# Top-32 attention with a SwiGLU block: ScalarE's part of the next two weight pieces put in front of exp

## The chip, the core and the metric

The kernel runs on one core of a Trainium2 chip. The core's engines run side by side, each through its own list of instructions in a fixed order, and wait for each other by semaphores: TensorE (PE in the profile; its weight loads are PEld), VectorE (DVE), ScalarE (ACT), GpSimd (POOL), and SyncE (SP), which here issues the transfers. The metric is the device time of one execution in microseconds, as the median over several executions. The time before is 1890.77 us (three executions, 1890.12 to 1893.95). The profile is of one further execution, whose span is 1892.5 us.

## The reference

Eight batches of eight heads, 576 positions, head size 64. Each row of scores keeps its 32 largest; the result, with the heads side by side, is the input of a feed-forward block of width 512 and inner width 1536.

```python
scores = scale * np.matmul(q, k.transpose(0, 1, 3, 2))
kth = np.partition(scores, -top_k, axis=-1)[..., -top_k:-top_k + 1]
scores = np.where(scores >= kth, scores, -1000000000.0)
attn = np.exp(scores - np.max(scores, axis=-1, keepdims=True))
attn = attn / (np.sum(attn, axis=-1, keepdims=True) + 1e-09)
x = np.matmul(attn, v)            # then (B,H,S,D) -> (B*S, H*D)
g = x @ w_gate
out = (g * (1.0 / (1.0 + np.exp(-g))) * (x @ w_val)) @ w_out
```

Here `top_k` is 32. The three weights come as 64-bit floats, each a low and a high 32-bit word, and everything is computed in 32-bit floats.

## The kernel before

**Units.** The attention is cut into 160 units `(b, qt, hp)`: a batch, a tile of 128 queries (or the last 64, a unit with half the work), and a pair of heads. The main loop is a software pipeline over units, and the program order of every engine is the order in which this loop writes its instructions down (a last pass ties each engine to it). In turn `n` of the loop:

- `penalize(n-1)` on GpSimd: a bias (L338) and the sum of scores and penalty (L340, 128x1152, the longest of GpSimd);
- `turn(n-3)`: transposes of the weights of attention on TensorE (L376) and their copies on ScalarE (L377); `finish_unit(n-4)`: the product with v (L396, L405) and the copy to `xT` (L420);
- the first step of `scores(n+1)`: matmuls (L297);
- `weigh(n-1)` on ScalarE: two exps with their row sums (L349) and a small addition (L354). It waits for L340;
- the rest of `scores(n+1)`: four copies of scores from PSUM on ScalarE (L302);
- `select(n)` on VectorE, step by step through `dve`: four rounds of MAX8 (L318) with three of MATCH_REPLACE8 (L322) for two heads, and at the end the penalties (L328). Between the steps stand pieces of the feed-forward block (`pieces`), the reciprocal and the scaling of unit `n-2` (`normalize`, L361 and L364), and steps of the weight pieces.

**Weight pieces.** Because the weights are 64-bit floats, the kernel itself turns them into 32-bit floats while the first units run. There are 72 pieces of 128x256; the generator `weights()` advances several of them by one step each in every one of its turns. `rounding(k)` runs k turns of it. `dve` calls `rounding(1)` in 5 of 11 of its counted steps, which is 4.5 pieces for a full unit. A piece goes through `rounded`:

1. SyncE loads it into `w`, a low and a high word for each element (L109);
2. ScalarE takes the absolute value of the high word (L114, into `size`); GpSimd clamps it (L116); ScalarE scales the low word by 2^-29 into a whole number (L119, into `ulps`);
3. VectorE shifts and masks `size` (L123); GpSimd adds `ulps` to it as whole numbers (L126);
4. VectorE puts the sign and top bit of the high word to it (L129). That is the finished weight, in `wg`, `wv` or `wo`.

The list `lags = (5, 3, 2, 0)` says how far apart these steps are: turn `n` finishes piece `n-5`, does step 3 of piece `n-3`, step 2 of piece `n-2`, and starts the transfer of piece `n`. So in every turn GpSimd has the addition L126 of piece `n-3` ahead of the clamp L116 of piece `n-2`, and VectorE has L129 ahead of L123. `size` has 4 buffers, `ulps` 2, `w` 6. Once all pieces are done, the same buffers hold differences of `wo` that the later blocks use (`t3`, `t2`, `t4`).

**Feed-forward blocks.** 18 blocks of 256 rows (`feed`), each a generator of small pieces of TensorE's work; `credit` sets how many of them a unit gets. A product's PSUM tile is emptied by ScalarE: for the gate a tanh, a halving and an addition (L484 to L486), for the value a copy (L491). The products with the gate and with the value are on GpSimd (L487, L492). Both kinds of work are put into the lists `on_act` and `on_pool`, and are written down when `flush` is called. The first block multiplies plainly by `w_out` (L505); the others use seven smaller products. `need` runs further turns of `weights()` if a block asks for a weight that isn't ready.

Before the loop:

```python
load(0)
rounding(4)
load(1)
run(fetch(0))
run(scores(0))
run(fetch(1))
```

Of the kernel before, what the change touches and what calls it, by code (L numbers as in the profile page):

```python
# [9 lines left out]
ALU = mybir.AluOpType  # L10
FP32 = mybir.dt.float32
I32 = mybir.dt.int32
U32 = mybir.dt.uint32
PSUM = bass.MemoryType.PSUM

P = 128
# [4 lines left out]
BLK = 256  # L21
# [6 lines left out]
def kernel(  # L28
# [37 lines left out]
    nc = tc.nc  # L66
    B, H, S, D = q.shape
    DM, DFF = w_gate.shape
# [6 lines left out]
    MS = MC // 2  # L75
# [10 lines left out]
    conv = ctx.enter_context(tc.tile_pool(name="conv", bufs=2))  # L86
# [18 lines left out]
    def rounded(src, dst):  # L105

        n = dst.shape[1]
        w = ffn.tile([P, n, 2], I32, tag="w", name="w", bufs=6)
        nc.sync.dma_start(w[:], src.bitcast(I32).rearrange("p (f t) -> p f t", t=2))  # L109
        yield  # L110
        low, high = w[:, :, 0], w[:, :, 1]

        size = conv.tile([P, n], FP32, tag="size", name="size", bufs=4)
        nc.scalar.activation(size[:], high.bitcast(FP32), AF.Abs)  # L114

        nc.gpsimd.tensor_scalar(size[:], size[:], HUGE, LEAST, ALU.min, ALU.max)  # L116

        ulps = conv.tile([P, n], I32, tag="ulps", name="ulps")
        nc.scalar.mul(ulps[:], low.bitcast(U32), 2.0**-29)  # L119
        yield  # L120

        bits = size[:].bitcast(I32)
        nc.vector.tensor_scalar(  # L123
            bits, bits, 3, 0x3FFFFFFF, ALU.logical_shift_left, ALU.bitwise_and
        )
        nc.gpsimd.tensor_tensor(bits, bits, ulps[:], ALU.add)  # L126
        yield

        nc.vector.scalar_tensor_tensor(  # L129
            out=dst.bitcast(I32), in0=high, scalar=-0x40000000, in1=bits,  # L130
            op0=ALU.bitwise_and, op1=ALU.bitwise_or,
        )

    def weights():

        pieces = []
        for f in range(0, DFF, WP):
            for src, dst in ((w_gate, wg), (w_val, wv)):
                for c in range(KC):
                    pieces.append((src[c * P : (c + 1) * P, f : f + WP], dst[:, c, f : f + WP]))  # L140
        for c in range(MC):
            for f in range(0, DM, WP):
                pieces.append((w_out[c * P : (c + 1) * P, f : f + WP], wo[:, c, f : f + WP]))
        pieces = [rounded(*p) for p in pieces]
        lags = (5, 3, 2, 0)
        for n in range(len(pieces) + lags[0]):
            for lag in lags:
                if 0 <= n - lag < len(pieces):
                    next(pieces[n - lag], None)
            ready[0] = max(n - lags[0] + 1, 0)  # L150
            yield


        add, sub = ALU.add, ALU.subtract
        lo, hi = slice(0, DM // 2), slice(DM // 2, DM)
        for m in range(0, MQ, 2):
            mm, nn = slice(m, m + 2), slice(MQ + m, MQ + m + 2)
            t3 = ffn.tile([P, 2, DM // 2], FP32, tag="w", name="t3", bufs=6)
            nc.gpsimd.tensor_tensor(t3[:], wo[:, nn, hi], wo[:, mm, hi], sub)
            T[7] += [t3[:, i, :] for i in range(2)]  # L160
            yield
        while not plain_done:
            yield
        for m in range(0, MQ, 2):
            mm, nn = slice(m, m + 2), slice(MQ + m, MQ + m + 2)
            t1 = wo[:, mm, hi]
            nc.gpsimd.tensor_tensor(t1, t1, wo[:, mm, lo], sub)
            T[5] += [wo[:, m + i, hi] for i in range(2)]
            yield
            t2 = ffn.tile([P, 2, DM // 2], FP32, tag="w", name="t2", bufs=6)  # L170
            nc.gpsimd.tensor_tensor(t2[:], wo[:, nn, hi], t1, sub)
            T[6] += [t2[:, i, :] for i in range(2)]
            yield
            for i in range(2):
                tag, bufs = ("size", 4) if m + i < 4 else ("ulps", 2)
                t4 = conv.tile([P, DM // 2], FP32, tag=tag, name="t4", bufs=bufs)
                nc.gpsimd.tensor_tensor(t4[:], wo[:, MQ + m + i, lo], t2[:, i, :], sub)
                T[4].append(t4[:])
            yield
        T[1] += [wo[:, m, lo] for m in range(MQ)]  # L180
        T[2] += [wo[:, MQ + m, lo] for m in range(MQ)]
        T[3] += [wo[:, MQ + m, hi] for m in range(MQ)]
        yield

    ready = [0]
    plain_done = []
    T = {i: [] for i in range(1, 8)}
    weight = weights()

    def rounding(n):  # L190
        for _ in range(n):
            next(weight, None)
# [70 lines left out]
    def n_heads(qt):  # L263

        return 1 if qt == J else 2
# [179 lines left out]
    def feed(kb):  # L445
# [5 lines left out]
        hs = []  # L451

        def product(w, s, then):
# [14 lines left out]
                yield 1  # L468

        plain = kb == 0  # L470
        early, late = slice(0, P), slice(P, BLK)

        s32 = x[:].rearrange("p a b -> p (a b)")[:, 0 : MQ * P].rearrange(
            "p (m t) -> p m t", t=P
        )
# [57 lines left out]
        def quarter(i, ps):  # L533
            for m in range(MQ):
                s, r = m // 2, m % 2
                lhsT = {
                    1: lambda: hs[s][:, r, early],
                    2: lambda: hs[s + MS // 2][:, r, early],
                    3: lambda: hs[s][:, r, late],
                    4: lambda: hs[s + MS // 2][:, r, late],  # L540
                    5: lambda: hs[s][:, r, late],
                    6: lambda: s32[:, m],
                    7: lambda: s32[:, m],
                }[i]()
                nc.tensor.matmul(  # L545
                    ps, lhsT, T[i][m], start=m == 0, stop=m == MQ - 1
                )
                if m % 3 == 2:
                    yield 0.75

        for s in range(MS // 2):
            nc.gpsimd.tensor_tensor(
                s32[:, 2 * s : 2 * s + 2], hs[s][:, :, early], hs[s][:, :, late], ALU.subtract
            )
        yield from quarter(1, y_ps[:, 0])
        flush(on_act)
# [6 lines left out]
        yield from quarter(7, x_ps[:, 1])  # L563
        for s in range(MS // 2):
            nc.gpsimd.tensor_tensor(
                s32[:, 2 * s : 2 * s + 2], hs[s][:, :, late], hs[s][:, :, early], ALU.subtract
            )
        yield from quarter(5, x_ps[:, 0])
        a = ffn.tile([P, 2, DH], FP32, tag="gv", name="p57", bufs=3)
# [22 lines left out]
        for s in range(MS // 2):  # L592
            nc.gpsimd.tensor_tensor(
                hs[s][:, :, late],
                hs[s + MS // 2][:, :, early],
                s32[:, 2 * s : 2 * s + 2],
                ALU.subtract,
            )
# [50 lines left out]
    def fetch(n):  # L649

        b, qt, hp = units[n]
        i = b * NHP + hp
        if qt == 0:
            yield from prep(i)
        if qt == J and i + NHP < len(pairs):
            load(i + NHP)
# [6 lines left out]
    def run(steps):  # L663
        for _ in steps:
            pass
# [5 lines left out]
            load_v((b + 1) * NHP + hp)  # L671

    load(0)
    rounding(4)
    load(1)
    run(fetch(0))
    run(scores(0))
    run(fetch(1))
    credit = [0.0]
    no = iter(())  # L680
# [3 lines left out]
    for n in range(NU + VALUES):  # L684
        nh = n_heads(units[n][1]) if n < NU else 1
        topk = select(n) if n < NU else no
        over[n - 1] = normalize(n - 1) if 0 <= n - 1 < NU else no
        nxt = scores(n + 1) if n + 1 < NU else no
        ahead = fetch(n + 2) if n + 2 < NU else no
        norm = over.pop(n - 2, no)  # L690

        def dve(k, beside=True):

            for _ in range(k * nh):
                next(topk, None)
                due[0] += 5 / 11 if beside else 0
                if due[0] >= 1:
                    due[0] -= 1
                    rounding(1)

        if n >= NU - NHP:
            credit[0] = 8.0
        else:
            credit[0] = min(credit[0] + (4.45 if nh == 2 else 2.25), 8.0)
        flush(on_act)
        if 0 <= n - 1 < NU:
            penalize(n - 1)
        flush(on_pool)
        if 0 <= n - TURN < NU:
            run(turn(n - TURN))  # L710
        if n >= VALUES:
            finish_unit(n - VALUES)
        next(nxt, None)
        if 0 <= n - 1 < NU:
            weigh(n - 1)
        run(nxt)

        dve(2, beside=False)
        if 2 <= n + 2 < NHP:
            load(n + 2)  # L720
        if n < NHP:
            load_v(n)
        pieces(2)
        flush(on_act)
        flush(on_pool)
        dve(1)
        dve(1)
        next(norm, None)
        run(norm)
        next(ahead, None)  # L730
        pieces(1)
        next(ahead, None)
        dve(1)
        pieces(1)
        dve(2)
        run(topk)
        pieces(6)
# [50 lines left out]
```

## Time and profile before

| | |
|---|---|
| time, median of 3 | 1890.77 us |
| span of the profiled execution | 1892.5 us |
| TensorE busy | 1723.2 us, 91% |
| VectorE busy | 1632.0 us, 86% |
| ScalarE busy | 1212.3 us, 64% |
| GpSimd busy | 1023.2 us, 54% |
| first and last Abs of a weight piece (L114) | 7.3 and 246.8 us |
| medians of L114, L116, L119, L123, L126, L129, us | 0.446, 0.400, 0.442, 0.288, 0.726, 0.41 |
| time that ScalarE waited before exp for L340 | 114.6 us in 49 waits, 66.2 of them before 480 us |

The profile's groups and waits are per engine: a busy time is a sum of the durations of instructions, and an idle time stands with the instruction that ended it and, behind an arrow, the one that released it. The timeline has a line for each instruction or run of like instructions: start, duration, engine, source line, operation, output and inputs, and in brackets the idle time before. Durations of neighbours on one engine overlap a little, so that the distance from start to start is shorter than the duration: two MAX8 of 0.75 us each together take 1.41.

### The profile page before, as it was taken

The numbers are of one execution on the slowest core, as the hardware profiler recorded it, in microseconds if no ns is written. First come the engines' busy times: TensorE is split into PE (matmuls) and PEld (weight loads), VectorE is DVE, ScalarE is ACT, GpSimd is POOL, SyncE is SP. The second block draws the span as 40 slices with busy tenths as digits, with TensorE's granted clock in tenths as the row PEclk, the third lists the DMA queues.
The fourth block names the chain that finished last, engine by engine and source line by source line (L and its number), as shares of the span: only waits on it lengthen the run. The fifth ranks groups of instructions, "written<-read, shape, count | busy, mean of one in ns | idle before, by whom it ended". The sixth has DMA issues, their size and how long they took to land.

```text
span 1892.5 us, 30875 instructions
## 1 busy us (share of the span) xinstructions
PE 1723.2 (91%) x10756; PEld 1419.1 (75%) x10756; DVE 1632.0 (86%) x3477; ACT 1212.3 (64%) x3015; POOL 1023.2 (54%) x1007
## 2 busy tenths in 40 slices
PE   3446789989999999899899999999999999899998
PEld 2335658868888878787788888878888878787877
DVE  7998789999999989997899989999899989999300
ACT  5656666667666666675667666766676767666531
POOL 4555656636455546555364655554646554546534
PEclk7668899989999999899999999999999999999989
DMA  7222212000300012000210003000210001000000
GB/s 186 84 84 78 67 27 69 1 12 2 78 12 12 1 28 64 12 1 13 52 38 1 12 3 82 7 12 1 53 38 12 1 14 46 18 1 12 1 12 12
DMA packets 111260, 59.67 MB, mean 32 GB/s; under 512 B 89088, under 2 KB 97280, under 8 KB 111104
## 3 DMA queue, kind: packets, MB, share of 16 engines
q1 hardware_dynamic: 109904, 57.41, 11.6%
q8 instruction: 85, 1.39, 0.3%
q14 instruction: 71, 0.58, 0.1%
q10 hardware_dynamic: 1200, 0.30, 0.1%
HBM read 48.23 MB, written 9.44 MB: 30 GB/s over the span
## 4 chain that ended last, share of the span: by engine, by line
PE 79%; ACT 7%; POOL 7%; DVE 4%; issue 2%; DMA 0%; SPq 0%; POOLq 0%; ACTq 0%
PE f L459 38%; PE av L405 8%; PE x_ps L545 8%; PE etps L376 8%; PE s L297 6%; PE y_ps L545 5%; POOL e L340 3%; ACT e L349 2%; PE s L283 2%; ACT sc L302 2%; PE av L396 1%; DVE m L318 1%; DVE rest L322 1%; PE kqps L252 1%; PE o_ps L505 1%
## 5 line engine op out<-in xcount | busy, mean ns | idle before, releaser
L318 DVE MAX8 m<-rest 128x8 f32<-128x576 f32 x864 | 615.2, 747 | 2.2
L322 DVE MATCH_REPLACE8 rest<-m,rest 128x576 f32<-128x576 f32 x576 | 423.9, 742 | 0.0
L340 POOL TENSOR_TENSOR e<-e,sc 128x1152 f32<-128x1152 f32 (+1 forms) x160 | 382.7, 2392 | 59.4 <-DVE e L328 59.0
L459 PE MATMUL f<-xT,wg 128*128 128x256 f32 x1728 | 404.8, 385 | 0.0
L459 PE MATMUL f<-xT,wv 128*128 128x256 f32 x1728 | 397.9, 381 | 0.0
L459 PEld LDWEIGHTS f<-xT,wg 128*128 128x128 f32 x1728 | 324.4, 191 | 66.7 <-issue 23.7
L459 PEld LDWEIGHTS f<-xT,wv 128*128 128x128 f32 x1728 | 324.3, 190 | 55.6 <-issue 13.5
L487 POOL TENSOR_TENSOR h<-h,half_g 128x512 f32<-128x512 f32 x108 | 138.0, 1278 | 385.9 <-ACT h L486 377.4
L318 DVE MAX8 m<-sc 128x8 f32<-128x576 f32 x288 | 205.4, 749 | 127.1 <-ACT sc L288 70.9
L376 PE MATMUL etps<-ident,e 128*128 128x128 f32 (+1 forms) x1312 | 191.0, 291 | 132.2 <-POOL size L116 48.1
L349 ACT ACTIVATE e<-e,bias 128x576 f32<-128x576 f32 x288 | 222.0, 776 | 114.6 <-POOL e L340 114.6
L376 PEld LDWEIGHTS etps<-ident,e 128*128 128x128 f32 (+1 forms) x1312 | 161.9, 150 | 163.9 <-POOL size L116 51.3
L377 ACT COPY et<-etps 128x512 f32<-128x512 f32 (+1 forms) x448 | 185.0, 483 | 126.5 <-PE etps L376 124.9
L492 POOL TENSOR_TENSOR h<-h,val 128x512 f32<-128x512 f32 x108 | 140.0, 1296 | 160.8 <-ACT val L491 160.8
L364 ACT ACTIVATE e<-e,tot 128x576 f32<-128x576 f32 x288 | 211.5, 787 | 5.3 <-DVE tot L361 5.1
L322 DVE MATCH_REPLACE8 rest<-m,sc 128x576 f32<-128x576 f32 x288 | 211.8, 741 | 0.0
L297 PE MATMUL s<-kqT 64*128 64x288 f32 x1024 | 175.5, 451 | 9.1 <-ACT kqT L257 5.8
L328 DVE TENSOR_SCALAR e<-sc,m 128x576 f32<-128x576 f32 x288 | 173.4, 639 | 3.4
L405 PE MATMUL av<-et,v 128*64 128x128 f32 (+1 forms) x2560 | 176.3, 284 | 0.0
L302 ACT COPY sc<-s 128x288 f32<-128x288 f32 x512 | 163.9, 402 | 3.3 <-PE s L297 3.3
L484 ACT ACTIVATE h<-f 128x512 f32<-128x512 f32 x108 | 65.2, 603 | 149.8 <-PE f L459 149.8
L405 PEld LDWEIGHTS av<-et,v 128*64 128x64 f32 x2560 | 139.2, 147 | 23.4 <-issue 7.9
(71 smaller groups left out, 2042.6 us busy)
## 6 DMA issues: line engine op xcount, KB each, us to landing
kq_in<-in_k_dram SPq DMA_DIRECT2D x64, 128.0 KB, 2.8
v<-in_v_dram SPq DMA_DIRECT2D x32, 256.0 KB, 3.0
kq_in<-in_q_dram SPq DMA_DIRECT2D x62, 128.0 KB, 2.9
w<-in_moe_w_gate_dram SPq DMA_DIRECT2D x24, 256.0 KB, 2.7
w<-in_moe_w_val_dram SPq DMA_DIRECT2D x24, 256.0 KB, 2.7
w<-in_moe_w_out_dram SPq DMA_DIRECT2D x24, 256.0 KB, 2.6
out_dram<-o SPq DMA_DIRECT2D x40, 128.0 KB, 2.4
out_dram<-o SPq DMA_DIRECT2D x16, 256.0 KB, 2.4
```

What stands on the lines that cost most here:

```text
L297: nc.tensor.matmul(ps[:, 0:half], slab[d, q0 : q0 + P], slab[d, k0 : k0 + half])
L302: nc.scalar.copy(sc[:, i * half : (i + 1) * half], ps[:, 0:half])
L318: nc.vector.max(m[:, t, 8 * r : 8 * r + 8], cur[:, hs])
L322: nc.vector.match_replace(rest[:, hs], m[:, t, 8 * r : 8 * r + 8], cur[:, hs], LOWEST)
L340: nc.gpsimd.tensor_tensor(e[:, every], e[:, every], sc[:, every], ALU.add)
L349: nc.scalar.activation(e[:, hs], e[:, hs], AF.Exp, bias=bias[:, t : t + 1], scale=scale, accum_out=tot[:, t : t + 1],)
L364: nc.scalar.mul(e[:, hs], e[:, hs], tot[:, t : t + 1])
L376: nc.tensor.transpose(ps[0:kl, c * P : (c + 1) * P], e[:, k0 : k0 + kl], ident[:])
L377: nc.scalar.copy(et[0:kl, c0 : c0 + cn, :], ps[0:kl, 0 : cn * P].rearrange("p (c j) -> p c j", c=cn),)
L405: nc.tensor.matmul(av[hh * R : (hh + 1) * R, 0:ql], v_last[:, hh, :] if c == J else vt[:, hh, c, :], moving, start=last and c == 0, stop=c ...
L459: nc.tensor.matmul(ps[:, i, :], w[:, kc, m * P : (m + 1) * P], x[:, kc, :], start=(kc == 0), stop=(kc == KC - 1),)
L545: nc.tensor.matmul(ps, lhsT, T[i][m], start=m == 0, stop=m == MQ - 1)
```

## The change

ScalarE's two instructions of a piece (L114 and L119) become a step of their own, ahead of the clamp. At the head of each unit, just before `weigh` writes the exps, the main loop calls `early[0]()`, which writes these two instructions for the last piece begun and the one before it; the other pieces are done in their usual turn, and what has been done early is not done again (`upto` counts the steps). It is meant to use the time in which ScalarE waits for L340, so that GpSimd's clamp doesn't have to wait for ScalarE after the exps and the copies of scores.

A piece's `size` is then in use for longer, and gets 6 buffers. The low word is scaled in place, in `w`, and the two `ulps` buffers are gone, so that the memory in use stays the same. Before the loop, two turns of `weights()` instead of four stand ahead of the first scores, and the other two after them. The slice `early` in `feed` becomes `first`, a change of name.

```diff
-        size = conv.tile([P, n], FP32, tag="size", name="size", bufs=4)
+        size = conv.tile([P, n], FP32, tag="size", name="size", bufs=6)
         nc.scalar.activation(size[:], high.bitcast(FP32), AF.Abs)

+        nc.scalar.mul(low, low.bitcast(U32), 2.0**-29)
+        yield
+
         nc.gpsimd.tensor_scalar(size[:], size[:], HUGE, LEAST, ALU.min, ALU.max)
-
-        ulps = conv.tile([P, n], I32, tag="ulps", name="ulps")
-        nc.scalar.mul(ulps[:], low.bitcast(U32), 2.0**-29)
         yield
...
-        nc.gpsimd.tensor_tensor(bits, bits, ulps[:], ALU.add)
+        nc.gpsimd.tensor_tensor(bits, bits, low, ALU.add)
...
-        lags = (5, 3, 2, 0)
+        step = [0] * len(pieces)
+
+        def upto(i, k):
+            while 0 <= i < len(pieces) and step[i] < k:
+                next(pieces[i], None)
+                step[i] += 1
+
+        lags = (5, 3, 2, 2, 0)
         for n in range(len(pieces) + lags[0]):
-            for lag in lags:
-                if 0 <= n - lag < len(pieces):
-                    next(pieces[n - lag], None)
+            for k, lag in enumerate(lags):
+                upto(n - lag, len(lags) - k)
             ready[0] = max(n - lags[0] + 1, 0)
+            early[0] = lambda: [upto(n - 1, 2), upto(n, 2)]
             yield
+        early[0] = lambda: None
...
-                tag, bufs = ("size", 4) if m + i < 4 else ("ulps", 2)
-                t4 = conv.tile([P, DM // 2], FP32, tag=tag, name="t4", bufs=bufs)
+                t4 = conv.tile([P, DM // 2], FP32, tag="size", name="t4", bufs=6)
...
     load(0)
-    rounding(4)
+    rounding(2)
     load(1)
     run(fetch(0))
     run(scores(0))
+    rounding(2)
     run(fetch(1))
...
         next(nxt, None)
+
+        early[0]()
         if 0 <= n - 1 < NU:
             weigh(n - 1)
         run(nxt)
```

More of the change, by code (lines that the diff above doesn't have):

```diff
@@ L185 @@
     ready = [0]
+    early = [lambda: None]
     plain_done = []
@@ L470, in feed @@
         plain = kb == 0
-        early, late = slice(0, P), slice(P, BLK)
+        first, late = slice(0, P), slice(P, BLK)
         s32 = x[:].rearrange("p a b -> p (a b)")[:, 0 : MQ * P].rearrange(
@@ L536, in quarter @@
                 lhsT = {
-                    1: lambda: hs[s][:, r, early],
-                    2: lambda: hs[s + MS // 2][:, r, early],
+                    1: lambda: hs[s][:, r, first],
+                    2: lambda: hs[s + MS // 2][:, r, first],
                     3: lambda: hs[s][:, r, late],
@@ L552, in feed @@
             nc.gpsimd.tensor_tensor(
-                s32[:, 2 * s : 2 * s + 2], hs[s][:, :, early], hs[s][:, :, late], ALU.subtract
+                s32[:, 2 * s : 2 * s + 2], hs[s][:, :, first], hs[s][:, :, late], ALU.subtract
             )
@@ L565, in feed @@
             nc.gpsimd.tensor_tensor(
-                s32[:, 2 * s : 2 * s + 2], hs[s][:, :, late], hs[s][:, :, early], ALU.subtract
+                s32[:, 2 * s : 2 * s + 2], hs[s][:, :, late], hs[s][:, :, first], ALU.subtract
             )
@@ L594, in feed @@
                 hs[s][:, :, late],
-                hs[s + MS // 2][:, :, early],
+                hs[s + MS // 2][:, :, first],
                 s32[:, 2 * s : 2 * s + 2],
```

## The prediction

> **What bounds the kernel now.** I read the 40 slices of the page first, then the busy time by stage, then the waits of VectorE, and last the timeline around two of these waits.
>
> ```profile
> PE   3446789989999999899899999999999999899998
> DVE  7998789999999989997899989999899989999300
> ACT  5656666667666666675667666766676767666531
> ```
>
> One digit is 47.3 us. TensorE is far from full in the first five or six slices and near full from there to the end. So there are two regimes, and the busy time of three stretches (columns: length, then busy PE, PEld, DVE, ACT, POOL, granted clock, DMA) says which engine leads in each:
>
> ```profile
> 12.79:165.00 152.21, 59.44 (x325) 45.85 (x325) 144.02 (x343) 94.17 (x254) 84.39 (x116) 0.65 0.38 107
> 165.00:255.00 90.00, 73.34 (x393) 57.38 (x395) 73.64 (x167) 57.42 (x143) 54.69 (x67) 0.92 0.19 58
> 500.00:1850.00 1350.00, 1314.13 (x8370) 1094.93 (x8369) 1182.49 (x2480) 881.39 (x2173) 725.85 (x667) 0.99 0.09 21
> ```
>
> From 12.79 us (first MAX8) to 165 VectorE works 144.0 of 152.2 us: it is the bound, and 8.2 us is all it idles. I call this stage A: attention units and weight pieces, with no feed-forward product yet. From 165 to 255 (stage B, the first feed-forward block beside the last pieces) it idles 16.4 us of 90, and no engine is full. After 255 TensorE leads, without weight pieces. Every engine runs a fixed program order, so time taken out before 255 moves all that comes later forward.
>
> Who ends VectorE's idle time:
>
> ```profile
> 60.07 0.29 DVE L123 TENSOR_SCALAR size<-size 128x256 int32<-128x256 int32 x1 [1.12 <-POOL size L116]
> 104.25 0.29 DVE L123 TENSOR_SCALAR size<-size 128x256 int32<-128x256 int32 x1 [0.80 <-POOL size L116]
> 117.74 0.29 DVE L123 TENSOR_SCALAR size<-size 128x256 int32<-128x256 int32 x1 [1.17 <-POOL size L116]
> 178.86 0.29 DVE L123 TENSOR_SCALAR size<-size 128x256 int32<-128x256 int32 x1 [3.23 <-POOL size L116]
> 230.91 0.29 DVE L123 TENSOR_SCALAR size<-size 128x256 int32<-128x256 int32 x1 [3.79 <-POOL size L116]
> ```
>
> It is always L123, the second of a unit, waiting for the clamp L116. In stage A there are ten such waits: 0.39, 0.29, 1.12, 0.81, 1.18, 0.80, 1.17, 0.81, 1.17, 0.45, together 8.19 us, which is the whole idle time of that stage. In stage B there are five: 3.23, 3.21, 3.01, 3.79, 3.11, together 16.35 us, again the whole. The two kinds have different causes. Stage A:
>
> ```profile
> 100.19 0.78 ACT L349 ACTIVATE e<-e,bias 128x576 f32<-128x576 f32 x1 [3.70 <-POOL e L340]
> 102.05 1.28 ACT L302 COPY sc<-s 128x288 f32<-128x288 f32 x4
> 103.20 0.46 ACT L114 ACTIVATE size<-w 128x256 f32<-128x256 f32 x1
> 103.82 0.40 POOL L116 TENSOR_SCALAR size<-size 128x256 f32<-128x256 f32 x1 [1.29 <-ACT size L114]
> 104.25 0.29 DVE L123 TENSOR_SCALAR size<-size 128x256 int32<-128x256 int32 x1 [0.80 <-POOL size L116]
> ```
>
> ScalarE stands idle 3.70 us before exp, then does exp, the score copies and only then Abs L114. The clamp waits 1.29 us for that Abs, and VectorE for the clamp. Stage B:
>
> ```profile
> 228.21 0.47 ACT L114 ACTIVATE size<-w 128x256 f32<-128x256 f32 x1
> 228.43 1.28 POOL L487 TENSOR_TENSOR h<-h,half_g 128x512 f32<-128x512 f32 x1 [3.52 <-ACT h L486]
> 229.66 0.73 POOL L126 TENSOR_TENSOR size<-size,ulps 128x256 int32<-128x256 int32 x1
> 230.47 0.40 POOL L116 TENSOR_SCALAR size<-size 128x256 f32<-128x256 f32 x1
> ```
>
> Here Abs ends at 228.68, long before the clamp. What holds GpSimd is the gate product L487, first in its queue, which waited 3.52 us for ScalarE's gate (L484 to L486, after exp and score copies); L126 and L116 stand behind it.
>
> **What the Trainium skill says.** "Perfetto Trace Analysis", Tensor Engine Instruction, says that ACT, DVE and GPSIMD are strict FIFO. The trace agrees: at 229.66 an add whose inputs had been ready for microseconds starts only when L487 ends. "GPSIMD Engine Reference", 7. Performance pitfalls, puts a cliff of +50% at SBUF reads of over 8 bytes step, and says that int32 step 2 is still below it. The new second operand of L126 (every other 32-bit word) is exactly at 8 bytes; no GpSimd instruction before reads with this step, so no run here shows it yet. "SBUF — State Buffer", Who interferes with whom, says that a VectorE instruction with two SBUF inputs contends with a GpSimd instruction that reads SBUF. The trace agrees: L129 (two inputs) takes 0.41 us in most places and 2.15 us at 188.13, while L340 ran from 187.38 to 190.00.
>
> **The change part by part.**
>
> *Two pieces' ScalarE part ahead of exp.* Four instructions (Abs and scale of pieces n-1 and n, n being the last piece begun) move to before exp. Back to back these start every 0.33 us (59.02, 59.35, 59.67, 59.99) and the last takes 0.45, so three times 0.33 plus 0.45 = 1.4 us. ScalarE's idle time before exp in the 16 units at 28 to 258 us is 5.08, 5.01, 4.32, 3.71, 3.85, 3.70, 3.36, 4.44, 3.44, 3.85, 3.72, 3.83, 3.24, 3.37, 3.25 and 3.17 us. The smallest leaves 1.7 us over, so exp is not late: cost nothing, hidden by the 2.62 us of L340 and the clamp and bias ahead of it.
>
> *The wait that this adds.* The first of the four can wait for a weight transfer; exp, the score copies and everything later on ScalarE are queued behind it. Piece n's transfer needs the buffer that L129 of piece n-6 frees. In the unit at 101 us, the L129s are at 101.06, 103.04, 105.85 and 108.50. Freed at 106.26 by the third, landing takes 2.7 us: 109.0; ScalarE gets there after 109.98 in this unit (exp at 113.68 less 3.36 idle is 110.32). Were it freed by the last (108.91), it would land at 111.6, and one piece's 0.8 us ends at 112.4, still before 113.68. Cost nothing at either end.
>
> *What it gives in stage A.* Without the wait for Abs, the clamp runs right after L126: in the unit shown 101.80 + 0.73 = 102.53, to 102.93. VectorE's L123 would be due at 104.25 - 0.80 = 103.45. Wait gone, 0.5 us to spare. In the other kind of unit, L126 starts 0.42 us after L123 (114.57, 114.99), and the clamp ends about 1.55 us after it, at 116.12; L123 is due at 117.74 - 1.17 = 116.57. Gone too. The next pieces of a unit have 1.93 us from one L123 to the next (104.25, 106.18) against 0.44 + 0.70 + 0.40 + 0.04 = 1.58 on GpSimd: no new wait. So all 8.19 us.
>
> *What it gives in stage B.* The clamp stays behind L487, whose release is exp, tot, score copies and gate on ScalarE, none of which moves. The five waits stay: 0. That the scale instruction no longer waits for a free "ulps" buffer (L119 behind L126, 15.5 us in 25 waits) shortens ScalarE's queue later in the unit; the instructions behind it (normalising, et copies) are not what VectorE waits for: 0.
>
> *In-place scale, six size buffers.* Same count of instructions and of buffers (4 + 2 before, 6 after). L119's write step and L126's read step become 8 bytes. L126 stays at 0.726 us by the skill's page; the upper end is its +50%, 1.09 us. The +0.36 would come twice a unit on stage B's chain (first L126 behind L487, last one ahead of L340), five units: 3.6 us; in stage A it eats the slack of 1.93 - 1.58 = 0.35 us and costs about nothing. I take 0 and keep 3.6.
>
> *The start.* ScalarE's pieces 0 and 1 (7.33 to 8.75 us) now come after the first score copies. The key and query copies can start at about 6.9 (transposes end 6.84) instead of 8.65, and scores about 1.4 us sooner. But L123 of piece 0 still stands before the first MAX8 on VectorE: score copies end at 13.06 - 1.4 = 11.7, Abs, clamp and L123 need 0.96 to L123 (7.33 to 8.29) plus 0.2, so MAX8 at 12.6 to 12.8 instead of 12.79: 0 to 0.2.
>
> *Renaming and the t4 buffers*: no instruction changes; nothing.
>
> Sum: -8.2 - 0.1 = -8.3 us; 1890.8 - 8.3 = 1882.5.
>
> **The rivals.**
>
> *A, the waits come back elsewhere (no change).* With VectorE never idle, L129 meets GpSimd instructions more often (two SBUF inputs), or L126 costs +0.36. For it: L129 lost 1.7 us at 188.13 in one meeting; clamp and L129#2 come within 0.1 us of each other (116.12, 116.16). Against: most L129 take 0.41 us. Half the gain lost and 3.6 us on stage B: 1890.8 - 4.1 + 3.6 = 1890.3.
>
> *B, slower: the step-2 operand is dear.* If L126 doubled (+0.73), stage B pays 2 x 5 x 0.73 = 7.3 us. In stage A each two-step gap lacks 0.73 - 0.35 = 0.38 us; with 4.5 pieces a unit at 2.2 steps each some 3.5 gaps are such, 1.3 us, ten units: 13. Net -8.2 + 7.3 + 13 = +12: 1903. Against it stands the page, which puts this step below the cliff.
>
> *C, more than forecast: stage B profits.* ScalarE has 1.3 us less in the middle of a unit. For it: scores wait for the et copies there, 2.43 us at 219.57. If that reached the chain in five units: 6.5 us more, 1876. Against: the chain from L340 to L487 runs ahead of all that moved.
>
> **How the numbers follow.** Forecast 0.64, A 0.17, B 0.09, C 0.10. The range 1876 to 1894 takes in the forecast, A and the near end of C, and leaves B out. Faster by over 0.2% (below 1887) is the forecast and C, plus the part of A that keeps some gain, less doubt on the sum: 0.76. Within 0.2%: 0.15. Slower: 0.09.
>
> **What would show it.** Right: L123 waits for L116 fall from 31.4 us in 16 to about 16 in five or six, all over 3 us, in the stretch of the first feed-forward block; VectorE idles under 2 us between its first MAX8 and the first feed-forward product; ScalarE's wait before exp falls to 2 to 3.5 us with the four instructions ahead of it; the L340s of stage A come every 13.5 us instead of 14.35 on average; L126 still 0.72 to 0.73 us. Wrong: exp starting later than the end of L340, L126 at 0.9 us or more, or stage B's waits below 3 us.

## The result, and the profile after

The changed kernel takes 1881.3 us (median of 6, 1877.86 to 1883.07) against 1891.2 us (median of 6); the ratio is 0.9942, with a 95% interval of 0.9929 to 0.9955. The forecast was 1882.5.

Most lines have new numbers in the changed source. Note that L116 and L119 have changed places:

| | before | after |
|---|---|---|
| Abs, shift and mask, addition, finished weight | L114, L123, L126, L129 | the same |
| clamp | L116 | L119 |
| scale of the low word | L119 | L116 |
| bias, sum of scores and penalty | L338, L340 | L347, L349 |
| exp, score copies | L349, L302 | L358, L311 |
| gate, its product, product with the value | L484 to L486, L487, L492 | L493 to L495, L496, L501 |
| penalties | L328 | L337 |

The 40 slices of the page of the changed kernel, TensorE, VectorE and ScalarE:

```profile
PE   3447789989999999899999999989999999899998
DVE  7998889998999989997899989999899989999300
ACT  5666657666766676575667676766776667676531
```

The picture is the one from before but for a few digits. A change of half a per cent is not to be seen here. The busy time from one L340 to another shows it (columns as in the prediction: length, then busy PE, PEld, DVE, ACT, POOL, granted clock, DMA). I take stage A from the L340 (after: L349) of the first unit to that of the eleventh, and stage B from there to that of the sixteenth. Before, stage A ran from 25.52 to 169.00:

```profile
25.52:169.00 143.48, 55.60 (x312) 43.23 (x313) 135.29 (x322) 89.05 (x239) 82.17 (x114) 0.63 0.36 100
```

After (the second line is stage B, 86.13 us before):

```profile
25.38:159.84 134.46, 54.82 (x318) 43.22 (x319) 134.16 (x322) 89.51 (x241) 82.77 (x114) 0.63 0.39 106
159.84:245.99 86.15, 66.48 (x365) 54.17 (x363) 69.79 (x159) 53.00 (x133) 52.17 (x63) 0.90 0.18 53
```

Stage A lost 9.02 us, with the same 322 VectorE instructions in both; VectorE now works 134.16 of 134.46 us. Stage B is as long as before, and VectorE idles 16.4 of its 86 us. These are the waits of VectorE after, all that the timeline shows from 13 to 245 us:

```profile
57.90 0.29 DVE L123 TENSOR_SCALAR size<-size 128x256 int32<-128x256 int32 x1 [0.30 <-POOL size L119]
169.72 0.29 DVE L123 TENSOR_SCALAR size<-size 128x256 int32<-128x256 int32 x1 [3.25 <-POOL size L119]
188.09 0.29 DVE L123 TENSOR_SCALAR size<-size 128x256 int32<-128x256 int32 x1 [3.21 <-POOL size L119]
205.88 0.29 DVE L123 TENSOR_SCALAR size<-size 128x256 int32<-128x256 int32 x1 [3.01 <-POOL size L119]
221.78 0.29 DVE L123 TENSOR_SCALAR size<-size 128x256 int32<-128x256 int32 x1 [3.78 <-POOL size L119]
239.66 0.29 DVE L123 TENSOR_SCALAR size<-size 128x256 int32<-128x256 int32 x1 [3.11 <-POOL size L119]
```

Of the ten waits of stage A one is left, at 0.30 us; the five of stage B stand there within 0.02 us. The same unit as in the prediction's first timeline, now (VectorE and GpSimd in one list, in order of time):

```profile
95.88 0.78 ACT L358 ACTIVATE e<-e,bias 128x576 f32<-128x576 f32 x1 [3.07 <-POOL e L349]
97.06 0.28 DVE L123 TENSOR_SCALAR size<-size 128x256 int32<-128x256 int32 x1
97.47 0.73 POOL L126 TENSOR_TENSOR size<-size,w 128x256 int32<-128x256 int32 x1 [1.63 <-ACT e L358]
98.29 0.40 POOL L119 TENSOR_SCALAR size<-size 128x256 f32<-128x256 f32 x1
99.05 0.28 DVE L123 TENSOR_SCALAR size<-size 128x256 int32<-128x256 int32 x1
```

The clamp L119 runs right behind L126 and ends at 98.69; the second L123 of the unit follows at 99.05 without a wait. Exp still waits for L349 and starts with its end.

What follows after 255 us is a plain shift in this pair. The L340 of the sixteenth unit comes 9.14 us earlier than before, that of the 110th 9.09 us. In the two profiled executions, whose spans are 12.7 us apart, the rest comes in two jumps, of 2.3 us at the 112th unit and 1.35 at the 148th. In the windows around the first one (before, then after) TensorE ran at a granted clock of 0.88 in the one and 1.00 in the other:

```profile
1256.00:1284.00 28.00, 25.89 (x147) 21.10 (x148) 28.00 (x64) 17.72 (x45) 9.59 (x8) 0.88 0.05 19
```
```profile
1247.00:1272.00 25.00, 21.98 (x141) 18.23 (x140) 25.00 (x55) 16.81 (x43) 8.96 (x8) 1.00 0.06 22
```

Neither jump goes with the change. From the L340 of the 111th unit to the next, before, e1 and e5 take 16.8 to 16.9 us, at a granted clock of 0.94, and the nine other kernels' traces take 14.5 us (clock 1.00 in after and after_again); e5 has the early step, and e9, which is among the nine, has not. From the 147th to the 148th unit the changed kernel itself took 14.46 us in one execution and 16.94 in the other (after_again). So 9.1 us belong to the change and the other 3.6 us of that pair don't.

### The profile page after: what moved, and what is told of

Same layout as the page of the kernel before. It is cut to its first block, busy times and chain, and to the rows that moved or that the text cites. A ratio compares the mean times of both kernels' runs of the same rounds, so it can differ in the third digit from the quotient of the medians.

```text
span 1879.8 us, 30848 instructions
## 1 busy us (share of the span) xinstructions
PE 1713.8 (91%) x10756; PEld 1413.8 (75%) x10756; DVE 1631.5 (87%) x3477; ACT 1210.3 (64%) x3015; POOL 1023.5 (54%) x1007
## 4 chain that ended last, share of the span: by engine, by line
PE 80%; DVE 6%; POOL 4%; ACT 3%; issue 3%; DMA 0%; POOLq 0%; ACTq 0%
PE f L468 39%; PE x_ps L554 8%; PE av L414 8%; PE etps L385 8%; PE s L306 6%; PE y_ps L554 5%; DVE m L327 2%; DVE rest L331 2%; PE s L292 2%; PE av L405 1%; POOL e L349 1%; PE kqps L261 1%; PE o_ps L514 1%; ACT e L358 1%; ACT sc L311 1%
## 5 line engine op out<-in xcount | busy, mean ns | idle before, releaser
L349 POOL TENSOR_TENSOR e<-e,sc 128x1152 f32<-128x1152 f32 (+1 forms) x160 | 382.7, 2392 | 59.5 <-DVE e L337 59.0
L468 PEld LDWEIGHTS f<-xT,wv 128*128 128x128 f32 x1728 | 324.3, 190 | 55.6 <-issue 13.5
L496 POOL TENSOR_TENSOR h<-h,half_g 128x512 f32<-128x512 f32 x108 | 137.9, 1277 | 383.6 <-ACT h L495 378.3
L358 ACT ACTIVATE e<-e,bias 128x576 f32<-128x576 f32 x288 | 222.0, 776 | 100.1 <-POOL e L349 100.1
L501 POOL TENSOR_TENSOR h<-h,val 128x512 f32<-128x512 f32 x108 | 139.6, 1293 | 159.9 <-ACT val L500 159.8
L337 DVE TENSOR_SCALAR e<-sc,m 128x576 f32<-128x576 f32 x288 | 173.9, 640 | 3.5
L306 PE MATMUL s<-kqT 64*128 64x288 f32 x1024 | 168.1, 444 | 3.9 <-ACT kqT L266 3.8
L311 ACT COPY sc<-s 128x288 f32<-128x288 f32 x512 | 163.8, 403 | 1.7 <-PE s L306 1.7
L493 ACT ACTIVATE h<-f 128x512 f32<-128x512 f32 x108 | 65.3, 604 | 147.8 <-PE f L468 147.8
```

What stands on the lines that cost most here:

```text
L306: nc.tensor.matmul(ps[:, 0:half], slab[d, q0 : q0 + P], slab[d, k0 : k0 + half])
L311: nc.scalar.copy(sc[:, i * half : (i + 1) * half], ps[:, 0:half])
L349: nc.gpsimd.tensor_tensor(e[:, every], e[:, every], sc[:, every], ALU.add)
L358: nc.scalar.activation(e[:, hs], e[:, hs], AF.Exp, bias=bias[:, t : t + 1], scale=scale, accum_out=tot[:, t : t + 1],)
L468: nc.tensor.matmul(ps[:, i, :], w[:, kc, m * P : (m + 1) * P], x[:, kc, :], start=(kc == 0), stop=(kc == KC - 1),)
```

## The experiments

All kernels' traces are read in the same way; the times are medians, the ratios, with their intervals, are against the kernel before on the same chip. They compare the whole sets of runs and need not be the quotients of the medians (for e1 that would be 0.9996). The experiments ran on three chips, where the kernel before had medians of 1893.1 us (e1 to e4), 1895.9 (after_again, e5 to e7) and 1892.9 (e8, e9), so that across these groups it is the ratios that compare.

| kernel | stage A, us | stage B, us | time, us | ratio (95%) |
|---|---|---|---|---|
| before | 143.48 | 86.13 | 1891.2 | 1 |
| after | 134.46 | 86.15 | 1881.3 | 0.9942 (0.9929 to 0.9955) |
| after_again | 134.48 | 86.21 | 1884.0 | 0.9943 (0.9928 to 0.9959) |
| e1_no_early | 143.21 | 86.29 | 1892.4 | 0.9985 (0.9973 to 0.9997) |
| e2_one_piece | 134.10 | 86.24 | 1883.0 | 0.9944 (0.9929 to 0.9959) |
| e3_behind_exp | 135.35 | 92.68 | 1888.9 | 0.9980 (0.9971 to 0.9988) |
| e4_more_act | 150.51 | 95.14 | 1907.4 | 1.0075 (1.0058 to 1.0091) |
| e5_clamp_early | 134.62 | 77.18 | 1874.8 | 0.9895 (0.9879 to 0.9911) |
| e6_clamp_one | 134.09 | 79.09 | 1876.4 | 0.9905 (0.9888 to 0.9921) |
| e7_gate_later | 134.46 | 73.85 | 1873.0 | 0.9885 (0.9868 to 0.9902) |
| e8_both | 134.59 | 72.14 | 1871.3 | 0.9886 (0.9867 to 0.9906) |
| e9_before_gate_later | 143.49 | 82.70 | 1889.0 | 0.9981 (0.9972 to 0.9990) |

**after_again: the changed kernel unaltered.** 

> The changed kernel unaltered, beside the next three on the same chip: about 1881, ratio 0.993 to 0.9955.

It is there for the comparison with the three kernels that ran beside it, and its stages agree with the first execution within 0.1 us.

**e1_no_early: everything but the step in front of exp.**

```diff
-            early[0] = lambda: [upto(n - 1, 2), upto(n, 2)]
+            early[0] = lambda: None
```

> The changed kernel without the instructions in front of exp: the in-place scale, the six size buffers and the new order at the start stay. Theory (the early ScalarE part is the whole gain): about 1891, within 0.2% of before; ten waits of L123 in stage A come back with about 8 us, L340 of the eleventh unit starts 0.1 to 0.5 us earlier than before's 169.0. Rival (the ulps buffers' wait or the start carried part of it): 3 us or more faster than before.

All ten waits of stage A are back (0.39, 0.29, 1.11, 0.82, 1.19, 0.82, 1.18, 0.82, 1.18, 0.46: 8.26 us), and so is the time of stage A. Two of them:

```profile
88.28 0.29 DVE L123 TENSOR_SCALAR size<-size 128x256 int32<-128x256 int32 x1 [1.19 <-POOL size L119]
103.64 0.29 DVE L123 TENSOR_SCALAR size<-size 128x256 int32<-128x256 int32 x1 [0.82 <-POOL size L119]
```

The eleventh unit's L349 is at 168.42, 0.6 us ahead of before's 169.00, half of it there already at the first unit's L349. In time the rest of the change is worth 0.15% (0.03 to 0.27); that interval reaches to 5 us and would not exclude the rival of 3 us or more. The stages do: stage A is 0.27 us shorter than before and stage B no shorter. The early step is what counts. Abs and scale moved together in every run; that Abs is the one of the two that matters is read from the waits (the clamp waits for L114), not tested.

**e2_one_piece: only the older piece in front of exp.**

```diff
-            early[0] = lambda: [upto(n - 1, 2), upto(n, 2)]
+            early[0] = lambda: [upto(n - 1, 2)]
```

> Only the older of the two pieces is done in front of exp. Theory: the wait in stage A hangs on the first clamp of a unit alone, since the second one stands behind the addition of its own turn; so the whole gain stays, about 1881, and the waits of L123 in stage A are under 1 us together. Rival (both pieces are needed): the next L123 of each unit waits instead, half the gain, about 1886.

Stage A has no wait of VectorE left at all. In the timeline of a unit the second piece's Abs comes behind the score copies:

```profile
97.81 0.40 POOL L119 TENSOR_SCALAR size<-size 128x256 f32<-128x256 f32 x1
98.41 0.47 ACT L114 ACTIVATE size<-w 128x256 f32<-128x256 f32 x1
98.57 0.28 DVE L123 TENSOR_SCALAR size<-size 128x256 int32<-128x256 int32 x1
98.99 0.74 POOL L126 TENSOR_TENSOR size<-size,w 128x256 int32<-128x256 int32 x1 [0.78 <-ACT size L114]
99.69 0.40 POOL L119 TENSOR_SCALAR size<-size 128x256 f32<-128x256 f32 x1
```

Abs ends at 98.88, and the clamp that needs it can't run before 99.69 in any case, since the addition L126, which needs L123 of 98.57, stands ahead of it. The second piece in front of exp is not needed for stage A.

**e3_behind_exp: the two pieces behind the exps.**

```diff
-        early[0]()
         if 0 <= n - 1 < NU:
             weigh(n - 1)
+        early[0]()
         run(nxt)
```

> The same two pieces behind the exps, still ahead of the score copies. Theory: in stage A Abs ends by the time the addition ahead of the clamp does, so stage A keeps its 9 us; in stage B score copies and gate come 1.3 us later, and GpSimd's gate product with them, so each of the five waits there grows by 1.3 us to about 4.5, 6.5 us in all: about 1888. Rival (the place against exp doesn't matter, only that against the score copies does): 1881.

Stage A keeps all but 0.9 us: three waits of 0.29, 0.29 and 0.30 are left. Stage B grows by 6.5 us, and the five waits are 4.58, 4.48, 4.31, 5.10 and 4.42, each 1.3 us over what they were. The timeline of the first:

```profile
165.03 0.43 ACT L114 ACTIVATE size<-w 128x256 f32<-128x256 f32 x1
166.34 1.28 ACT L311 COPY sc<-s 128x288 f32<-128x288 f32 x4
168.46 0.67 ACT L495 ACTIVATE h<-h 128x512 f32<-128x512 f32 x1
169.21 1.28 POOL L496 TENSOR_TENSOR h<-h,half_g 128x512 f32<-128x512 f32 x1 [6.07 <-ACT h L495]
170.44 0.74 POOL L126 TENSOR_TENSOR size<-size,w 128x256 int32<-128x256 int32 x1
171.27 0.40 POOL L119 TENSOR_SCALAR size<-size 128x256 f32<-128x256 f32 x1
171.71 0.29 DVE L123 TENSOR_SCALAR size<-size 128x256 int32<-128x256 int32 x1 [4.58 <-POOL size L119]
```

The 1.3 us between the first Abs and the score copies goes link by link to VectorE. For nearly all of stage A's gain it is enough that Abs comes ahead of the score copies; that it comes ahead of exp is what keeps stage B free of cost.

**e4_more_act: how much fits in front of exp.** Each early piece takes its Abs seven times; the repeats write the same values.

```diff
-        nc.scalar.activation(size[:], high.bitcast(FP32), AF.Abs)
+        for _ in range(7 if heavy[0] else 1):
+            nc.scalar.activation(size[:], high.bitcast(FP32), AF.Abs)
```

> Each of the two early pieces does its Abs seven times instead of once: 12 more ScalarE instructions, 4.0 us, in front of exp in each of 16 units. Theory: ScalarE's time before exp that is left is 2 to 3 us in stage A and 2.7 to 4.8 in stage B, so exp comes 0 to 2 us late; stage A hides that (up to 2 us in all), stage B pays it, about 0.9 us in four of five units: about 1885, 3 to 6 us over the changed kernel. Rival (exp isn't on the path in stage B either): 1881. Rival (no slack in stage A): 10 us or more over the changed kernel.

Stage B pays, as expected, but 9.0 us; stage A pays 16 us, far from hidden. With 25 us over the changed kernel the rival without slack (10 us or more) is nearer than my theory. ScalarE's part of the timeline in one unit of stage A shows why:

```profile
98.73 3.26 ACT L115 ACTIVATE size<-w 128x256 f32<-128x256 f32 x7
101.90 0.42 ACT L117 ACTIVATE w<-w 128x256 int32<-128x256 uint32 x1
102.22 3.22 ACT L115 ACTIVATE size<-w 128x256 f32<-128x256 f32 x7
105.35 0.42 ACT L117 ACTIVATE w<-w 128x256 int32<-128x256 uint32 x1
105.67 0.76 ACT L360 ACTIVATE e<-e,bias 128x576 f32<-128x576 f32 x1
```

The sum of scores and penalty (here L351) had ended at 102.2; exp is 3.5 us late, and in the ten units of stage A 2.1 to 5.3 us. Two terms of my theory were off. Seven Abs in a row start every 0.47 us and not every 0.33, so that twelve more are 5.6 us in a unit instead of 4.0; and the changed kernel has 1.0 to 3.2 us left before exp in stage A, not 2 to 3. What ScalarE does later in the unit, the Abs of the other pieces behind exp and score copies among it, is then late too, and the old wait is back:

```profile
126.14 0.40 POOL L120 TENSOR_SCALAR size<-size 128x256 f32<-128x256 f32 x1 [3.41 <-ACT size L115]
126.58 0.29 DVE L124 TENSOR_SCALAR size<-size 128x256 int32<-128x256 int32 x1 [3.00 <-POOL size L120]
```

Stage A has twelve such waits of VectorE for the clamp, together 15.4 us, which is nearly all of its 16. Besides, ScalarE is now busy 137.0 us of stage A, from 26.2 to 176.7 us. In the changed kernel it was busy 89.5, and 137.0 is more than the whole 134.46 us of the stage there: so much work would not have fitted anywhere. How much of the 16 us comes from the overfilled gap before exp and how much from the full engine, this run does not separate.

**e5_clamp_early and e6_clamp_one: the clamp at the unit's head too.** GpSimd then has it behind L340 and ahead of the gate product.

```diff
-            early[0] = lambda: [upto(n - 1, 2), upto(n, 2)]
+            early[0] = lambda: [upto(n - 1, 3), upto(n, 3)]
```

e6 has `upto(n - 1, 3), upto(n, 2)`.

> The clamps of both early pieces go to the unit's head too, so that on GpSimd they stand behind L340 and ahead of the gate product. Theory (stage B's wait is the clamp's place behind the gate product): the five waits of L123 over 3 us are gone; the next thing that VectorE needs from behind the gate product is the addition, two turns later, about 1 us of wait; so some 2 us less a unit in stage B, 8 to 10 us in all, and stage A as it is: about 1872. Rival (L129 with two inputs meets the clamps on GpSimd, up to 0.4 us in each of 16 units): gain in stage B but 3 to 6 us given back in stage A, about 1877. Rival (stage B is bound by TensorE's products and ScalarE): the waits move, 1881.

> Only the older piece's clamp goes to the head. Theory: the second clamp is needed after the addition of the first turn anyway, so this gives what both clamps give, about 1872, with less to meet for L129.

e5 takes 9.0 us out of stage B and leaves stage A as it was. What is left is the addition behind the gate product, as worked out, in five waits of 0.17 to 1.18 us (4.1 us together). One of them:

```profile
169.56 0.95 DVE L129 SCALAR_TENSOR_TENSOR wo<-w,size 128x256 int32<-128x256 int32 x1 [1.18 <-POOL size L126]
```

The waits shrink by 12.3 us, but VectorE's 159 instructions of stage B now take 73.1 us instead of 69.8, so that 9.0 us remain. Five L129 of some 0.95 us, begun 0.1 us after the start of an addition on GpSimd, make 2.7 of these 3.3 us (most L129 take 0.41). The rival of such meetings was right in kind, though in stage B and not in stage A.

e6 gives 7.1 us in stage B; it has the same waits of L129 and another 0.29 us at an L123 in each unit. So by the stages the second clamp is worth 1.9 us, against what I expected; in time e5 and e6 can't be told apart (0.9895 and 0.9905).

**e7_gate_later: the gate product behind the clamp.** On GpSimd the first turn's addition and clamp come ahead of L496.

```diff
         pieces(2)
         flush(on_act)
-        flush(on_pool)
         dve(1)
         dve(1)
+        flush(on_pool)
```

> GpSimd's gate product is written down behind two further VectorE steps instead of ahead of them, so that the first turn's addition and clamp stand ahead of it; nothing else changes place. Theory: the five waits over 3 us shrink to under 0.5, the gate product starts up to 1 us later, which TensorE doesn't need soon; stage B then is near full on TensorE (66.5 us of products in 86), so of the 16 us of waits 8 to 12 come out: about 1871. Rival (TensorE needs the gate product soon, or is the bound): 1878 to 1881.

Stage B shrinks by 12.3 us to 73.85. Two waits of L123 are left, of 1.00 and 1.01 us, where I expected all under 0.5. The first of them in its unit:

```profile
165.03 0.74 POOL L126 TENSOR_TENSOR size<-size,w 128x256 int32<-128x256 int32 x1 [2.35 <-ACT sc L311]
165.85 0.40 POOL L119 TENSOR_SCALAR size<-size 128x256 f32<-128x256 f32 x1
166.60 0.28 DVE L123 TENSOR_SCALAR size<-size 128x256 int32<-128x256 int32 x1
167.44 1.28 POOL L496 TENSOR_TENSOR h<-h,half_g 128x512 f32<-128x512 f32 x1 [1.19 <-ACT h L495]
170.00 0.29 DVE L123 TENSOR_SCALAR size<-size 128x256 int32<-128x256 int32 x1 [1.00 <-POOL size L119]
```

Addition and clamp run in the time in which GpSimd had waited for the gate, and the gate product starts when the gate is done. With 1873.0 us it is 11 us ahead of the changed kernel on the same chip.

**e8_both: e5 and e7 together.** 

> Both early clamps at the unit's head and the gate product behind two further VectorE steps. Theory: with the gate product later, VectorE has only two waits of 1.0 us left in stage B, so at most 2 us more than with the gate product alone: 1871 to 1873, or the same. Rival (clamps at the head meet L129): 1875.

Stage B is 1.7 us shorter than e7's and has no wait of VectorE left (busy 72.14 of 72.14 us); in time the two can't be told apart (0.9886 and 0.9885).

**e9_before_gate_later: e7's edit in the kernel before.** 

> The kernel before with only the gate product later. Theory: in stage B its clamp then no longer stands behind the gate product but still waits for Abs, which ScalarE does after the gate (Abs ends at 176.6 in the unit at 169, the clamp ended at 178.8): so each of the five waits shrinks by about 1.8 us to 1.2 to 2, 8 to 9 us in all, and stage A keeps its ten waits: about 1882. With the early ScalarE part as well the same move gave 11 us. Rival (the place of the gate product is all of stage B's wait): 1879.

Stage A is before's 143.5. The waits in stage B shrink, to 1.61, 1.50, 1.37, 3.13 and 1.49, 9.1 us instead of 16.35: four of them by 1.6 to 1.7 us, about as expected, and one by 0.7. But stage B gets only 3.4 us shorter, and the time of 1889 us missed the 1882 that I expected. VectorE's busy time took the rest back: the same 159 instructions took 69.77 us in before's stage B and 73.60 here, since the later gate product on GpSimd now meets L123 (twice) and L129 (three times). One of each:

```profile
177.47 0.40 POOL L116 TENSOR_SCALAR size<-size 128x256 f32<-128x256 f32 x1 [2.08 <-ACT size L114]
177.84 1.27 POOL L487 TENSOR_TENSOR h<-h,half_g 128x512 f32<-128x512 f32 x1
177.91 1.36 DVE L123 TENSOR_SCALAR size<-size 128x256 int32<-128x256 int32 x1 [1.61 <-POOL size L116]
```

```profile
197.14 1.28 POOL L487 TENSOR_TENSOR h<-h,half_g 128x512 f32<-128x512 f32 x1
197.24 1.46 DVE L129 SCALAR_TENSOR_TENSOR wo<-w,size 128x256 int32<-128x256 int32 x1
```

L123 took 1.36 us instead of 0.29, twice, which is 2.1 us; L129 took 1.46, 0.74 and 0.74 us instead of 0.41, which is 1.7. Together that is the 3.8 us between the waits and the stage. The two moves help each other: in the changed kernel the later gate product brings 12.3 us in stage B, without the early Abs 3.4.

## Why the prediction was right

*VectorE bounds stage A and idles only for the clamp.* Right: with nine of the ten waits gone VectorE is full, and e1, which puts Abs back, brings the ten waits and the 9 us back.

*8.2 us in stage A.* Right in mechanism, 0.8 us too small. The idle time fell by 7.89 us (8.19 less the 0.30 that is left); the other 1.13 of the 9.02 us is busy time, 135.29 us before and 134.16 after for the same 322 instructions. The idle time in brackets counts from the end of the instruction before, but neighbours on VectorE overlap: L129 to L123 was 0.69 us from start to start in before's unit at 46.30 and is 0.33 after, 0.36 less for a wait shown as 0.29. Some 0.08 us at each wait that is gone is 0.7 to 0.8 us. Another 0.36 us is a pair of penalties in the third unit that took 1.52 us before and 1.16 after. The 0.30 that is left is a place where the clamp and an L129 both start at 57.19 and the clamp takes 0.68 us instead of 0.40: rival A's meeting, the only one that made a wait.

*Nothing in stage B.* Right to 0.02 us. That its cause is the clamp's place behind the gate product, whose own release is exp, score copies and gate, is shown from both sides: e3 makes the gate 1.3 us later and each wait 1.3 us longer, and e7 takes the clamp out from behind the product and 12.3 us with it. Rival C (less ScalarE work in the middle of a unit helps stage B) brought nothing. The 0.02 is closer than the traces repeat: after_again's stage B is 0.08 us longer than before's.

*The early step is hidden in front of exp.* Right as a statement, since exp starts at the end of L349 in every unit that has weight pieces in front of it. The time left over is less regular than I said: 1.0 to 4.8 us where I named 2 to 3.5, and in four units ScalarE waits for a piece's transfer there, 2.25 us at most (at 210.64), with 3.15 us still to spare. e4 put 5.6 us more into it, and the waits came back.

*The in-place scale costs nothing.* L126 has a median of 0.736 us against 0.726, ScalarE's scale 0.428 against 0.442. This agrees with the Trainium skill, "GPSIMD Engine Reference", 7. Performance pitfalls, which puts a read step of 8 bytes still below the cliff; the +0.36 of rival A (an estimate from that page's +50%) and the +0.73 of rival B did not come.

*The start.* 0.14 us in this pair, within 0 to 0.2, but that is not shown: the first L349 is at 25.38 us in after and at 25.58 in after_again, which is later than before's 25.52.

*All of it arrives at the end.* Right: the shift is 9.1 us from the eleventh unit to the 110th, through 1000 us in which TensorE leads. That it stays so even is in part luck of the pair: two units in between, the 31st and the 67th, are 1.0 and 1.2 us longer in before and after alike and not in after_again. The ratio of the times, 0.58% (0.45 to 0.71) or 8.5 to 13.4 us, agrees with it; the 8.3 us that were forecast lie just under this interval, by about what stage A was sized too small.

*The signs.* The waits of L123 for the clamp fell from 15 with 24.5 us to six with 16.7 us, as said. The prediction's "31.4 us in 16" also counts one of 6.88 us at 8.29, ahead of the first MAX8, which is 11.03 us after; it lies outside both stages and says nothing of the change's gain. The L340s of stage A come every 13.45 us, where 13.5 was named, and L126 is with 0.736 us a little over the 0.72 to 0.73.

## What to carry to other kernels

Ask for each wait of the bounding engine what stands ahead of its releaser in that engine's queue: the same wait (L123 for the clamp) had one cause in stage A and another in stage B, and only the first was cured by this change. Put the side work of an engine where it waits for something long, ahead of the link that others wait for; one piece done early in each unit was enough here (e2). Idle time in front of one instruction is less room than it looks: what goes in must fit the smallest gap, at the pace at which it really runs, and the engine's whole period must have room for it too. e4 broke all of this at once and doesn't say what each part costs. When an instruction is moved to another place in its queue, look at what it will run beside there: in e9 meetings with GpSimd's gate product took back half of what VectorE's shorter waits gave.

## What the runs showed of the hardware

VectorE and GpSimd can stretch each other where they meet, and not only at VectorE instructions with two inputs from SBUF. In e9, L123, with one input, took 1.36 us instead of 0.29 when the gate product had started 0.07 us earlier, and ended 0.16 us after it. The Trainium skill, "SBUF — State Buffer", Who interferes with whom, counts single-input tensor-scalar instructions among those that can take the port pair shared with GpSimd, if their operands meet certain conditions, and this agrees with it. The prediction had reckoned with L129 alone, though before's trace has such an L123 too, of 1.36 us at 190.20, begun 0.24 us after a product with the value. In e5 L129 took 0.95 us instead of 0.41 right behind the start of an addition on GpSimd, and in e7 2.18 us beside the sum L349.
